# The heads' operand buffers moved into a pool of their own, released after the experts

## The chip, the cores and the metric

The kernel runs on one core of one Trainium2 chip. The metric is device time in microseconds of that core for one execution; the span of the profile, from its first to its last instruction (672.7 us for an execution of 674.4 us) is a little shorter. Five engines run side by side[...]: TensorE (PE, products), VectorE (DVE), ScalarE (ACT), GpSimd (POOL) and SyncE (SP, which here issues most DMA transfers).

## The reference

A gated linear attention (4 batches, 8 heads, 768 steps, head width 48, a complex gate) is followed by a mixture of 8 experts that sends each of the 3072 rows to one expert. Cut to what matters:

```python
def _attn_ref(q, k, v, a_re, a_im):
    mag = np.sqrt(a_re * a_re + a_im * a_im)
    scale = np.minimum(mag, 0.999) / (mag + 1e-06)
    a_re_n, a_im_n = (a_re * scale, a_im * scale)
    for t in range(S):                       # S = 768
        ...                                  # complex state, one step
        S_re, S_im = (new_re + kv, new_im)
        y[:, :, t] = np.einsum('bhd,bhde->bhe', q[:, :, t], S_re)

def _moe_ref(x, w_gate, w1, w2):             # x: 3072 rows of 384, from y
    logits = x @ w_gate
    expert_idx = np.argmax(logits, axis=1)
    ...                                      # gate_w: softmax weight of the chosen expert
    for e in range(E):                       # E = 8
        xe = x[expert_idx == e]
        h = np.maximum(xe @ w1[e], 0.0)      # 384 -> 1024
        out[mask] = gate_w[mask, None] * (h @ w2[e])
```

## The kernel before

Attention works in chunks of 128 steps. For each head it builds two operands, `KX` (keys and the chunk's decay) and `QX` (queries and a scaled diagonal), in a ring of six buffers each. The finished rows are collected in `xf`, given an expert and a place, and scattered by indirect DMA into `sorted_x` in HBM, expert by expert. The experts then load their rows from there, transpose them on VectorE, and multiply twice on TensorE. All of attention's tiles, the rings too, come from one pool, `one`:

```python
    with ExitStack() as att:
        one = att.enter_context(tc.tile_pool(name="one", bufs=1))
        ...
        def buf(nm, *shape):
            return one.tile([128, *shape], FP32, name=nm)
        ...
        packs = [buf(f"pk{i}", 2, C * CW) for i in range(3)]
        ...
        KXs = [buf(f"KX{i}", C * CW) for i in range(RING)]
        QXs = [buf(f"QX{i}", C, 128 + R2) for i in range(RING)]
        for i in range(RING):
            P.memset(KXs[i][R2:128, :], 0.0)
            P.memset(QXs[i][R2:128, :, :], 0.0)
```

The first 256 rows of expert 0 come from the first three batches, so they are complete before the last batch is. They are done early, between attention's last products: `early()` keeps their hidden values and results in operand buffers of heads that are through (`hq`, `hk`, `ys`), and writes the results to `out` from there:

```python
        def early(weights_in):
            w1t, w2t = weights(0)
            slots = [heads[B - 1, h][0] for h in (2, 3)]
            ...
            hq, hk = QXs[slots[0]].rearrange("p c w -> p (c w)"), KXs[slots[0]]
            ht = [...]                                   # eight slices of hq and hk
            ys = [KXs[slots[1]][:, i * DM:i * DM + DM] for i in range(EARLY // 128)]
            ...
            for i in range(EARLY // 128):
                ...                                      # products with w2 into o_ps
                o = act(DM, lambda i=i, o_ps=o_ps: A.activation(ys[i], o_ps, func=ACT.Copy, scale=gt_e[:, i, 0:1]), ...)
                pool_dma(1.1, lambda i=i: to_out(ys[i], out, to_e[:, i:i + 1]), [o, to])
```

The recorded operations (their source line is always that of one helper, L136) are put in an order by a scheduler of the kernel's own and emitted. Then the pool `one` is given back, and the experts open theirs. Expert 0 has only its late rows left there, 192 of its 448 places:

```python
    with ExitStack() as ms:
        xp = ms.enter_context(tc.tile_pool(name="xp", bufs=2))
        ...
        def load(e):
            xq = xp.tile([128, CAP // 32, R2], FP32, name="xq")
            c0 = first_tile(e) * 4
            for u in range(4):
                nc.sync.dma_start(xq[u * 32:u * 32 + 32, c0:], blocks(e, u, c0 * 32, CAP))   # L868
            return xq, notes_of(e)
        ...
        def turned(e, xq):
            xt = mp.tile([128, DT, CAP], FP32, name="xt")
            for d in range(DT):
                c0 = first_tile(e) * 4
                nc.vector.transpose(xt[:, d, c0 * 32:]..., xq[:, c0:, d * 32:d * 32 + 32])   # L885
            return xt

        xq, gt = load(0)
        mp = ms.enter_context(tc.tile_pool(name="mp", bufs=2))
        xt = turned(0, xq)
        for e in range(E):
            if e + 1 < E:
                xq, gt_next = load(e + 1)
            ...
            for f in range(FT):                          # first product and relu
                h = bank_of("h")[:, cols]
                for d in range(DT):
                    T.matmul(h, lhsT=w1t[:, d, f * 128:f * 128 + 128], rhs=xt[:, d, cols], ...)
                if f % 2:
                    nc.vector.tensor_scalar_max(ht[:, f, cols], h, 0.0)                      # L906
                else:
                    nc.scalar.activation(ht[:, f, cols], h, func=ACT.Relu)                   # L908
            if e + 1 < E:
                xt = turned(e + 1, xq)
            ...                                          # second product, results yo
            y = mp.tile([128, HALF], FP32, name="yh", bufs=2)
            nc.vector.tensor_scalar_mul(y, o[:, 0:HALF], gt[:, TT, 0:1])                     # L927
            to_out(y, halves, to[:, TT:TT + 1])
            if e + 3 < E:
                fetch(e + 3, nc.sync)                    # weights into the buffer of expert e
    banks.close()
```

A tile in a pool that takes over given-back memory waits for the users of the pool that it takes over from. TensorE's instructions keep their program order here (`T` is an in-order wrapper); VectorE's and ScalarE's in this part may be moved past each other when the program is built.

Of the kernel before, what the change touches and what calls it, by code (L numbers as in the profile page):

```python
# [9 lines left out]
FP32 = mybir.dt.float32  # L10
# [9 lines left out]
C = S // 128  # L20
# [6 lines left out]
CW = 128 + 2  # L27
R2 = 2 * D
RING = 6
# [110 lines left out]
def gateloop_then_moe(ctx, tc, q, k, a_re, a_im, v, wg, w1, w2, out):  # L140
# [142 lines left out]
    banks = ExitStack()  # L283
    bank = banks.enter_context(tc.tile_pool(name="bank", bufs=1, space=PSUM))
    two = bank.tile([128, 1024], FP32, name="two")
    ps = [two[:, 0:512], two[:, 512:]] + [bank.tile([128, 512], FP32, name=f"bank{i}") for i in range(2, 8)]

    with ExitStack() as att:
        one = att.enter_context(tc.tile_pool(name="one", bufs=1))
        V, A, T, Q = (InOrder(tc, e) for e in (nc.vector, nc.scalar, nc.tensor, nc.sync))  # L290
# [8 lines left out]
        def buf(nm, *shape):  # L299
            return one.tile([128, *shape], FP32, name=nm)  # L300
# [29 lines left out]
        P.memset(xfs[ROWS - 1][:, 0:XD + 1], 0.0)  # L330
        P.memset(xfs[ROWS - 1][:, XD + 1:WS], 4.0 * N)

        KXs = [buf(f"KX{i}", C * CW) for i in range(RING)]
        QXs = [buf(f"QX{i}", C, 128 + R2) for i in range(RING)]
        for i in range(RING):
            P.memset(KXs[i][R2:128, :], 0.0)
            P.memset(QXs[i][R2:128, :, :], 0.0)
# [773 lines left out]
```

## Time and profile before

| | |
|---|---|
| times of three runs | 676.70, 672.72, 676.45 us; median 676.45 |
| span of the profiled run | 672.7 us, 8204 instructions |
| busy TensorE / VectorE / ScalarE / GpSimd | 550.1 / 369.2 / 289.4 / 79.4 us |
| mean granted TensorE clock | 0.921 |
| moved by DMA | 89.81 MB, mean 134 GB/s |

The page gives the span in 40 slices with a digit for each engine's busy share in tenths, and groups of instructions: line, engine, operation, written tile <- read tiles, count, then busy time, mean ns of one, and the idle time of the engine just ahead of them with what ended it. In the timeline a row is the start, the duration, the engine, the line, the operation with its tiles, and in brackets the idle time ahead of it and what released it. `SPq` and `POOLq` stand for the issue of a DMA transfer by SyncE or GpSimd, not for its movement of data. Every product of fp32 tiles appears as two matmuls.

### The profile page before, as it was taken

To read this page: it belongs to the slowest core of one execution; us is meant where nothing else is said; L and a number is where in the kernel's file an instruction comes from. 1 tells how busy PE (TensorE), PEld (TensorE's weight loads), DVE (VectorE), ACT (ScalarE), POOL (GpSimd) and SP (SyncE) were. 2 spreads that over 40 slices of the span, in tenths; PEclk is the share of its full clock that TensorE was granted. 3 is DMA by queue.
4 is the path that set the end of the run, shared out by engine and by line. 5 is a ranking of instruction groups with operands and counts; after the bars stand their busy time and mean duration, and the time that the engine had idled before them with its cause. 6 is when DMAs were issued, how large, how long until landed. Compare 5 with 4: busy or idle time off the path is not lost. (4 is left out here: it accounts for less than half of the span.)

```text
span 672.7 us, 8204 instructions
## 1 busy us (share of the span) xinstructions
PE 550.1 (82%) x2594; PEld 336.1 (50%) x2594; DVE 369.2 (55%) x782; ACT 289.4 (43%) x940; POOL 79.4 (12%) x96
## 2 busy tenths in 40 slices
PE   1550388968897778977998689999999999999993
PEld 0220245645564455654666375555555565655552
DVE  5999999999999999999533021201111201110010
ACT  6555588688998697766642001000000001010100
POOL 9100000000004004004003101110101020101111
PEclk9666599979999698979999989999999999999997
DMA  8694857277635646287397156354434441000000
GB/s 258 154 246 114 205 133 200 65 197 172 159 95 143 166 122 184 58 202 184 93 366 287 34 131 157 126 151 136 142 116 137 97 120 75 24 18 24 9 12 29
DMA packets 77635, 89.81 MB, mean 134 GB/s; under 512 B 25341, under 2 KB 67343, under 8 KB 75536
## 3 DMA queue, kind: packets, MB, share of 16 engines
q1 hardware_dynamic: 74000, 79.33, 43.6%
q0 software_dynamic: 3584, 9.87, 4.1%
q8 instruction: 22, 0.36, 0.2%
q14 instruction: 29, 0.24, 0.1%
HBM read 54.31 MB, written 16.63 MB: 105 GB/s over the span
## 5 line engine op out<-in xcount | busy, mean ns | idle before, releaser
L136 PE MATMUL bank<-xt,big 128*128 128x448 f32 (+1 forms) x384 | 137.7, 520 | 8.1 <-DVE xt L885 8.1
L136 PE MATMUL bank<-big,ht 128*128 128x384 f32 (+1 forms) x608 | 136.8, 420 | 0.0
L136 PE MATMUL bank<-QX,KX 128*128 128x224 f32 (+1 forms) x384 | 95.5, 382 | 34.7 <-DMA KX<-pk 26.1
L136 PEld LDWEIGHTS bank<-big,ht 128*128 128x128 f32 (+1 forms) x608 | 84.5, 168 | 53.6 <-issue 7.0
L136 PEld LDWEIGHTS bank<-xt,big 128*128 128x128 f32 x384 | 72.6, 194 | 70.5 <-issue 61.6
L136 PEld LDWEIGHTS bank<-QX,KX 128*128 128x128 f32 x384 | 69.3, 207 | 51.6 <-issue 34.7
L136 ACT ACTIVATE big<-big 128x576 f32<-128x576 f32 (+3 forms) x77 | 68.6, 904 | 15.6 <-DVE big L136 14.2
L906 DVE TENSOR_SCALAR ht<-bank 128x448 f32<-128x448 f32 (+1 forms) x32 | 18.9, 591 | 100.0 <-PE bank L136 100.0
L136 ACT ACTIVATE QX<-diag,KX 96x48 f32<-96x48 f32 x280 | 72.6, 336 | 1.6 <-DMA KX<-pk 1.6
L908 ACT ACTIVATE ht<-bank 128x448 f32<-128x448 f32 (+1 forms) x32 | 16.6, 518 | 130.5 <-PE bank L136 120.5
L785 POOL DMA_INDIRECT sorted_x<-xf,slot x24 | 30.4, 1265 | 316.7 <-DMA big<-in_a_im_dram 154.6
L136 PE MATMUL two<-big,ident 128*128 128x512 f32 (+1 forms) x112 | 42.0, 527 | 30.1 <-ACT big L136 25.7
L136 PE MATMUL bank<-ak,vb 128*48 128x224 f32 (+1 forms) x384 | 54.8, 369 | 14.0 <-ACT ak L136 12.1
L136 DVE TENSOR_TENSOR big<-big,big 128x576 f32<-128x576 f32 (+3 forms) x86 | 65.0, 766 | 0.8
L919 ACT ACTIVATE yo<-bank,gt 128x384 f32<-128x384 f32 x15 | 8.7, 582 | 122.4 <-PE bank L136 122.4
L136 DVE TENSOR_TENSOR big<-big 128x288 f32<-128x288 f32 (+5 forms) x108 | 55.2, 519 | 6.2 <-ACT big L136 5.5
L269 POOL DMA_INDIRECT out_dram<-yo,to x22 | 21.3, 970 | 239.4 <-ACT yo L919 183.5
L136 DVE TENSOR_TENSOR ak<-bank,causal 128x256 f32<-128x256 f32 x96 | 39.9, 418 | 15.9 <-PE bank L136 15.3
L136 PEld LDWEIGHTS two<-big,ident 128*128 128x128 f32 x112 | 21.9, 229 | 50.0 <-issue 32.7
L136 PE MATMUL bank<-QX,st 128*48 128x224 f32 (+1 forms) x320 | 44.0, 355 | 0.8 <-ACT st L136 0.8
L136 PE MATMUL bank<-across,ys 128*128 128x104 f32 x192 | 38.2, 290 | 4.4 <-ACT xf L136 2.3
L136 ACT ACTIVATE ys<-bank 128x224 f32<-128x224 f32 (+1 forms) x96 | 32.4, 344 | 18.1 <-PE bank L136 17.6
(126 smaller groups left out, 556.4 us busy)
## 6 DMA issues: line engine op xcount, KB each, us to landing
big<-in_moe_w_dram SPq DMA_DIRECT2D x16, 1536.0 KB
KX<-pk SPq DMA_DIRECT2D x44, 146.2 KB
QX<-pk SPq DMA_DIRECT2D x44, 144.0 KB
sorted_x<-xf SPq DMA_DIRECT2D x8, 731.5 KB
xq<-sorted_x SPq DMA_DIRECT2D x28, 168.0 KB
big<-in_a_re_dram SPq DMA_DIRECT2D x16, 288.0 KB
big<-in_a_im_dram SPq DMA_DIRECT2D x16, 288.0 KB
qt<-in_q_dram SPq DMA_DIRECT2D x12, 384.0 KB
```

Source lines behind the costliest of these rows:

```text
L136: return lambda *a, **kw: self.tc.keep_in_program_order(f(*a, **kw))
L269: move = nc.gpsimd.indirect_dma_start(out=rows, out_offset=bass.IndirectOffsetOnAxis(ap=index, axis=0), in_=y, in_offset=None, bounds_chec ...
L785: move = nc.gpsimd.indirect_dma_start(out=sorted_x[:, :], out_offset=bass.IndirectOffsetOnAxis(ap=slot[:, i:i + 1], axis=0), in_=xfs[(b * ...
L906: nc.vector.tensor_scalar_max(ht[:, f, cols], h, 0.0)
L908: nc.scalar.activation(ht[:, f, cols], h, func=ACT.Relu)
L919: nc.scalar.activation(y, o, func=ACT.Copy, scale=gt[:, i, 0:1])
```

## The change

The rings of `KX` and `QX` go into a pool of their own, opened ahead of attention's pool and closed only after the experts (with the PSUM banks, `banks.close()`). It is meant so that late rows' buffers in the experts' pools wait only for attention's other tiles, not for the operands, in which the early rows' results still stand. No instruction is added or taken away in the source.

```diff
@@ -285,6 +285,9 @@
     two = bank.tile([128, 1024], FP32, name="two")
     ps = [two[:, 0:512], two[:, 512:]] + [bank.tile([128, 512], FP32, name=f"bank{i}") for i in range(2, 8)]
 
+
+    ring_of = banks.enter_context(tc.tile_pool(name="ring", bufs=1))
+
     with ExitStack() as att:
         one = att.enter_context(tc.tile_pool(name="one", bufs=1))
         V, A, T, Q = (InOrder(tc, e) for e in (nc.vector, nc.scalar, nc.tensor, nc.sync))
@@ -330,8 +333,8 @@
...
-        KXs = [buf(f"KX{i}", C * CW) for i in range(RING)]
-        QXs = [buf(f"QX{i}", C, 128 + R2) for i in range(RING)]
+        KXs = [ring_of.tile([128, C * CW], FP32, name=f"KX{i}") for i in range(RING)]
+        QXs = [ring_of.tile([128, C, 128 + R2], FP32, name=f"QX{i}") for i in range(RING)]
         for i in range(RING):
             P.memset(KXs[i][R2:128, :], 0.0)
             P.memset(QXs[i][R2:128, :, :], 0.0)
```

## The prediction

> **What bounds the kernel now.** I read the busy times by slice first, then one table by stretch of time for the hand-over from attention to experts, then the waits, then the timeline there. Part 2 of the page says that two engines take turns: VectorE is at 9 tenths or more up to about half the span, TensorE after it.
>
> ```profile
> PE   1550388968897778977998689999999999999993
> DVE  5999999999999999999533021201111201110010
> PEclk9666599979999698979999989999999999999997
> ```
>
> Counted from 1, each slice is 16.8 us long; slice 23 shows a 6 for TensorE, the lowest digit between the middle of the span and its last slice. The table by stretch puts edges to it (columns: stretch and its length, busy us of each engine with instruction counts, granted clock, DMA share, GB/s):
>
> ```profile
> 368.00:381.00 13.00, 11.88 (x41) 6.98 (x40) 1.00 (x3) 1.35 (x3) 0.97 (x1) 1.00 0.05 17
> 381.00:389.10 8.10, 0.03 (x1) 0.00 (x0) 0.41 (x2) 0.58 (x1) 0.97 (x1) 0.77 0.26 61
> 389.10:391.60 2.50, 2.48 (x8) 2.48 (x9) 0.68 (x4) 0.03 (x1) 0.00 (x0) 0.50 0.84 171
> 391.60:398.70 7.10, 7.10 (x43) 7.10 (x42) 1.07 (x3) 1.30 (x4) 0.00 (x0) 0.95 0.28 37
> 420.00:662.00 242.00, 241.91 (x861) 135.63 (x860) 33.94 (x70) 21.75 (x39) 26.19 (x27) 1.00 0.29 84
> ```
>
> From 381.0 to 389.1 TensorE does nothing; in the 2.5 us after that it has half its clock; from 420 to 662 it is busy for 241.91 of 242 us. So whatever starts the experts earlier ends the kernel earlier. Who holds it back: first the row of part 5 for the experts' first product (its last column: idle before, and what ended it), then the waits of the DMA queue and of all engines from 366 to 410.
>
> ```profile
> L136 PE MATMUL bank<-xt,big 128*128 128x448 f32 (+1 forms) x384 | 137.7, 520 | 8.1 <-DVE xt L885 8.1
> ```
>
> ```profile
> SPq L868 <- DMA out_dram<-KX,to_e: 43.6, 2, 39.8
> ...
> DVE xt L885 <- DMA xq<-sorted_x: 13.1, 1, 13.1
> ```
>
> The chain is: product waits for the transposed rows xt, xt for the load xq, and the load for the DMA that writes the early rows' result out of a KX buffer. That store has nothing to do with the rows being loaded. The timeline has the moments:
>
> ```profile
> 375.12 0.42 DVE L136 TENSOR_SCALAR KX<-two 128x256 f32<-128x256 f32 x1 [4.97 <-PE two L136]
> 378.93 2.10 PE L136 MATMUL two<-big,KX 128*128 128x384 f32 x6
> 381.92 0.97 POOL L269 DMA_INDIRECT out_dram<-KX,to_e  x1 [2.85 <-ACT KX L136]
> 384.82 1.78 SPq L868 DMA_DIRECT2D xq<-sorted_x  x4
> 388.69 0.90 DVE L885 STREAM_TRANSPOSE xt<-xq 128x192 f32<-128x192 f32 x3 [13.15 <-DMA xq<-sorted_x]
> 389.12 9.60 PE L136 MATMUL bank<-xt,big 128*128 128x192 f32 x48 [8.10 <-DVE xt L885]
> 399.03 1.69 DVE L885 STREAM_TRANSPOSE xt<-xq 128x448 f32<-128x448 f32 x3
> 406.56 18.31 PE L136 MATMUL bank<-xt,big 128*128 128x448 f32 x48
> 406.68 0.42 DVE L927 TENSOR_SCALAR yh<-bank,gt 128x192 f32<-128x192 f32 x1 [5.96 <-PE bank L136]
> ```
>
> The second early store is issued at 381.92, and the loads of xq start at 384.82, 2.9 us later; 3.87 us from there to the transposes, 0.43 more to the product.
>
> **What the Trainium skill says.** (1) "TensorE: Matmul & The Clock Gate", Part 1: the clock halves after an idle window of about 3.4 us and comes back after about that much sustained work. The trace agrees: 0.77 over the 8.1 us of idleness, 0.50 in the 2.5 us after it. (2) "DMA: Bandwidth & Descriptors", Anatomy of one DMA (SWDGE): some 2 us are fixed for a DMA issued by GpSimd, most of it the receipt of the write. Here 2.9 us from issue to the waiter, of which 0.97 us are GpSimd's own. (3) The TensorE page again, Architectural detail: VectorE's queue is strictly first in, first out. That matters for the part of the change that I count as a cost; nothing in the timeline above contradicts it.
>
> **The change part by part.** I laid the two built programs side by side, engine by engine, with what each instruction waits for. Every engine has as many instructions as before, and their order is the same except for four on VectorE.
>
> (a) Memory. KX and QX take 51,072 bytes of each partition. Before they lie behind the other attention tiles, after in front of them. The experts' tiles move up by the same 51,072 bytes, so that they lie on the same attention tiles as before (rows on the old state, packing and value tiles; the half-row result on the edge of xf). They never lay on KX or QX: the wait came from giving back one pool as a whole, with every user of it.
>
> (b) Waits removed. The first xq load, the first transpose, the first expert product and the first relu lose the wait for the two early stores and for the activation that fills KX. What the load keeps: the six last scatters into sorted_x (it reads what they write) and attention's last uses of other tiles. The last scatter is issued at 365.54; from 368 to 370 the DMA moves 0 GB/s, so it has landed by about 368. Loads start there, and with the same 3.87 us xq is in by 372.2. VectorE must first do its last early relu, 375.12 + 0.42; then three transposes in 0.90 us: xt is there by 376.5. TensorE ends the early rows at 378.93 + 2.10 = 381.03. So xt is 4.5 us ahead and the product follows at once: **-8.1 us**.
>
> (c) Clock. With no idleness the experts' first stage runs at full clock. In the timeline its relus come every 0.975 us once the clock is back (392.90 on VectorE to 398.75, six stages in 5.85 us). Eight stages then take 7.8 us; before they took 389.12 to 398.55, 9.43 us: **-1.6 us**.
>
> (d) Order on VectorE. The scale of expert 0's half rows (yh) stands ahead of the three transposes for expert 1 now; before it stood behind them. yh waits for the last product of expert 0, and expert 1's first product waits for the first transpose. Before, the transposes ran at 399.03, hidden; after, they lie between two products. yh begins 0.12 us after the last product (406.68 against 406.56) and takes 0.42; a transpose 0.60 (the median of the 21 of this width); 0.1 us from a transpose's end to the product (388.69 + 0.335 for the shorter form = 389.03, product at 389.12). Sum 0.12 + 0.42 + 0.60 + 0.1 = 1.2 us. The second and third transposes come 0.55 us apart (1.69 for three), the products on each third take 2 x 0.375 = 0.75 us, so only the first one shows: **+1.2 us**. It happens at expert 0 alone.
>
> (e) The start. The initial clears of KX and QX on GpSimd, and the first load of q, exchange a wait on the setup tiles. Those are done by 3.5 us, and the engines reach these instructions at 6.2 us or later: 0.
>
> Sum: -8.1 - 1.6 + 1.2 = -8.5 us. The median before is 676.45, which gives 667.95. The three times before are 672.72, 676.45 and 676.7; their mean, 675.3, gives 666.8. I choose 667.5.
>
> **The rivals.** *The next wait takes over.* If the scatters land late, or the loads queue behind the 9.4 MB of weights that share the queue, xt comes after 381. For: the loads stand behind those in program order. Against: DMA share is 0.30 from 366 to 368 and 0 after it, and 4.5 us are in hand. Were xq to land at 385, the product would start at 385.4: 3.7 us of the idleness gone, the slow clock still there after 4.4 us without work, and (d) to pay: -2.5, some 674.
> *The order on VectorE costs more.* A stall of 1.2 us could pull the clock down for a window: another 1.7 us (3.4 us at half clock), some 669. Against: before, TensorE's stall of 1.02 us ahead of the early product at 364.36 leaves the clock at 1.00.
> *The gain is lost later.* The weights of expert 3 are loaded into buffers that expert 0 frees; all that moves earlier by the same amount. For losing it a wait would have to exist after 420, and TensorE lacks only 0.09 us there, with DMA share 0.29. Nothing to lose it to; this would make 676.
>
> **Range and chances.** The change in time is -8.5, with -10 if the stall hides and -2.5 if the loads come late. The larger uncertainty is the 4 us between runs of one program. So 663.5 to 670.5. Two per cent of 676.45 is 13.5 us: faster by that would need more than all of the idleness and the slow clock together (9.7 us), 0.04; slower would need a new wait of over 22 us, 0.02; within, 0.94.
>
> **What would show it.** Right: the wait of L868 on the store from KX is gone and one on the scatters stands in its place; xq starts near 368, xt near 375.5; TensorE's idleness of 8.1 before the first xt product is gone, and an idleness of about 1.2 us, ended by a VectorE transpose, appears near 397; clock 1.00 from 381 on; the last product ends about 8.5 us earlier. Wrong: xq starting later than 377, the clock at 0.5 after 381, or an idle TensorE behind expert 1.

## The result, and the profile after

| | median of four runs, us | lowest to highest |
|---|---|---|
| before | 675.56 | 672.72 to 676.70 |
| after | 665.62 | 664.63 to 666.24 |

The ratio is 0.9858, with a 95% interval of 0.9822 to 0.9893: 9.9 us less by these medians. Two further comparisons, each beside its own runs of the kernel before, gave 0.9864 (0.9844 to 0.9885) and 0.9859 (0.9835 to 0.9882), that is 9.2 and 8.8 us. The prediction was 667.5, 8.5 us less.

First, part 2 of the page of after, in the same 40 slices:

```profile
PE   1541288968899478968998999999999999999993
...
PEclk9865599998999689988999999999999999999997
```

TensorE's hole of slice 23 has become a 9, as in all slices behind it up to the last. The table by stretch (columns as before: stretch and length, busy us of TensorE, its weight load, VectorE, ScalarE and GpSimd, the granted clock, the DMA share, GB/s) covers the end of the early rows, expert 0's first stage, the join to expert 1 and the long rest:

```profile
379.10:381.60 2.50, 2.50 (x15) 2.23 (x14) 0.00 (x0) 0.91 (x2) 0.86 (x1) 1.00 0.00 0
381.60:388.00 6.40, 6.40 (x40) 6.27 (x39) 1.39 (x4) 0.99 (x3) 0.11 (x1) 1.00 0.08 31
...
395.00:400.00 5.00, 3.85 (x17) 2.00 (x14) 2.13 (x6) 0.54 (x1) 0.97 (x1) 1.00 0.73 246
410.00:652.00 242.00, 242.00 (x862) 135.77 (x860) 33.81 (x69) 21.73 (x39) 26.24 (x27) 1.00 0.29 84
```

The idleness ahead of expert 0 is gone and the clock is 1.00 throughout. Of the stretches shown, only that from 395 to 400 has a gap: 5.00 - 3.85 = 1.15 us. The row of part 5 for the experts' first product says what ends it, and the waits of the DMA queue say what the load of xq waits for now:

```profile
L136 PE MATMUL bank<-xt,big 128*128 128x448 f32 (+1 forms) x384 | 136.1, 514 | 1.1 <-DVE xt L888 1.1
```

```profile
SPq L871 <- DMA sorted_x<-xf,slot: 27.2, 1, 27.2
```

L871 is the xq load, which was L868 before. It no longer waits for the store out of KX, only for the scatters into the rows that it reads. The timeline of after:

```profile
364.36 0.97 POOL L788 DMA_INDIRECT sorted_x<-xf,slot  x1 [2.81 <-issue]
367.86 1.78 SPq L871 DMA_DIRECT2D xq<-sorted_x  x4
...
374.64 0.90 DVE L888 STREAM_TRANSPOSE xt<-xq 128x192 f32<-128x192 f32 x3 [0.27 <-issue]
...
377.75 2.10 PE L136 MATMUL two<-big,KX 128*128 128x384 f32 x6
379.69 7.96 PE L136 MATMUL bank<-xt,big 128*128 128x192 f32 x48
380.74 0.97 POOL L269 DMA_INDIRECT out_dram<-KX,to_e  x1 [2.85 <-ACT KX L136]
387.49 8.07 PE L136 MATMUL bank<-big,ht 128*128 128x384 f32 x48
...
395.68 0.42 DVE L930 TENSOR_SCALAR yh<-bank,gt 128x192 f32<-128x192 f32 x1 [7.64 <-PE bank L136]
396.02 1.69 DVE L888 STREAM_TRANSPOSE xt<-xq 128x448 f32<-128x448 f32 x3
...
396.71 5.53 PE L136 MATMUL bank<-xt,big 128*128 128x448 f32 x14 [1.15 <-DVE xt L888]
```

The load is issued 13 us ahead of the store it used to wait for (367.86 against 380.74), and the transposed rows are there at 375.54, 4.2 us before TensorE asks for them. At 395.68 VectorE scales the half rows first and transposes second; expert 1's product waits 1.15 us for that.

One difference between the two profiles is not the change's. Expert 0's product starts 9.43 us sooner, but 1.06 us of that was already there at the first scatter of the last group (356.12 before, 355.06 after), in a part of the program that does the same work. Over all profiles below this moment lies anywhere between 355.06 and 358.64. So I measure from it. The table gives, for each profiled execution, the start of the first scatter of that group, and the times from it to expert 0's first product, through expert 0's first stage, from its second stage to expert 1's first product, and from there to the end of the span. Each is the difference of two starts in the timeline; the last stretch ends with the span. The kernels that follow "after" are explained with the experiments.

| kernel | first scatter | to expert 0 | its first stage | second stage to expert 1 | to the end | scatter to expert 1 |
|---|---|---|---|---|---|---|
| before | 356.12 | 33.00 | 9.43 | 8.01 | 266.1 | 50.44 |
| before, again | 356.69 | 33.19 | 9.50 | 8.00 | 266.1 | 50.69 |
| after | 355.06 | 24.63 | 7.80 | 9.22 | 266.2 | 41.65 |
| after, second time | 356.50 | 24.73 | 7.80 | 9.22 | 266.4 | 41.75 |
| after, third time | 357.26 | 24.69 | 7.80 | 9.22 | 266.4 | 41.71 |
| wait put back | 355.65 | 32.03 | 10.28 | 8.01 | 266.4 | 50.32 |
| only KX moved | 355.64 | 27.42 | 7.91 | 8.00 | 266.1 | 43.33 |
| only QX moved | 357.17 | 33.21 | 9.98 | 8.01 | 266.2 | 51.20 |
| before, kept busy | 356.50 | 33.14 | 7.91 | 8.00 | 266.7 | 49.05 |
| order fixed | 356.92 | 24.72 | 7.80 | 8.01 | 266.2 | 40.53 |
| order fixed, again | 358.64 | 24.72 | 7.80 | 8.01 | 266.4 | 40.53 |
| four areas, own schedule | 355.94 | 29.17 | 9.55 | 8.01 | 266.3 | 46.73 |
| four areas, old schedule | 356.81 | 22.35 | 7.80 | 8.00 | 266.2 | 38.15 |

From before to after: 33.1 to 24.7 is -8.4, 9.47 to 7.80 is -1.7, 8.0 to 9.22 is +1.2, and nothing behind it: -8.9 us together (50.57, the mean of the two profiles of before, to 41.70). The medians of the three comparisons gave 8.8 to 9.9 us.

### The profile page after: what moved, and what is told of

It reads as the page before. It is cut to its first block, busy times and chain, and to the rows that moved or that the text cites. A ratio compares the mean times of both kernels' runs of the same rounds, so it can differ in the third digit from the quotient of the medians.

```text
span 662.9 us, 8204 instructions
## 1 busy us (share of the span) xinstructions
PE 547.0 (83%) x2594; PEld 334.5 (50%) x2594; DVE 368.9 (56%) x782; ACT 289.4 (44%) x940; POOL 79.0 (12%) x96
## 5 line engine op out<-in xcount | busy, mean ns | idle before, releaser
L136 PE MATMUL bank<-xt,big 128*128 128x448 f32 (+1 forms) x384 | 136.1, 514 | 1.1 <-DVE xt L888 1.1
L136 PEld LDWEIGHTS bank<-xt,big 128*128 128x128 f32 x384 | 71.1, 190 | 63.3 <-issue 60.8
```

What stands on the lines that cost most here:

```text
L136: return lambda *a, **kw: self.tc.keep_in_program_order(f(*a, **kw))
```

## The experiments

My theory: the one wait that the pool's giving back put on xq made all of the idleness, the idleness made the slow clock, and the order on VectorE costs 1.2 us. The rivals: the memory's places or the changed program itself make the gain; the clock has nothing to do with it; the 1.2 us stall is made up later.

### The changed kernel again, and its VectorE order mended

> The changed kernel itself, as the measure for the others on this chip. 665.6 us, within 1 us. Its profile is a second sample of the attention phase: in the first, TensorE ended the early rows 1.2 us earlier than in the kernel before (379.85 against 381.03), though nothing in that phase was changed. If that is chance, this run's early rows end anywhere from 379.5 to 381.5; if the new addresses make attention faster, near 379.8 again.

> The changed kernel with the transposes for the next expert kept ahead of the half rows' scale on VectorE, by program order. Theory (the stall of 1.15 us between expert 0 and expert 1 is the price of the new order): that idleness of TensorE is gone and the time is 1.1 us below the changed kernel's, 664.5. Rival (the products would wait for something else there, such as the load of xq for expert 1 or the results' PSUM bank): a stall of about the same length with another releaser, 665.6.

The second kernel keeps the transposes and the scale in program order, so that the transposes run while expert 0's second products do:

```diff
+        V = InOrder(tc, nc.vector)
-                nc.vector.transpose(xt[:, d, c0 * 32:]..., xq[:, c0:, d * 32:d * 32 + 32])
+                V.transpose(xt[:, d, c0 * 32:]..., xq[:, c0:, d * 32:d * 32 + 32])
-            nc.vector.tensor_scalar_mul(y, o[:, 0:HALF], gt[:, TT, 0:1])
+            V.tensor_scalar_mul(y, o[:, 0:HALF], gt[:, TT, 0:1])
```

Measured: 666.37 us (665.25 to 668.35) for the changed kernel, 665.28 us (664.7 to 667.01), ratio 0.9848 (0.9833 to 0.9863), for the mended one. Its timeline:

```profile
389.44 8.07 PE L136 MATMUL bank<-big,ht 128*128 128x384 f32 x48
...
389.92 1.69 DVE L136 STREAM_TRANSPOSE xt<-xq 128x448 f32<-128x448 f32 x3
...
397.45 10.79 PE L136 MATMUL bank<-xt,big 128*128 128x448 f32 x28
397.64 0.42 DVE L136 TENSOR_SCALAR yh<-bank,gt 128x192 f32<-128x192 f32 x1 [6.03 <-PE bank L136]
```

The transposes start 7.5 us before the product that needs them (389.92 against 397.45), and the product has no idle time ahead of it. In the table the second stage falls from 9.22 to 8.01 us, and nothing behind it gives the 1.21 us back. By the medians it is 1.1 us here and 0.6 in the last comparison below; these intervals alone do not separate the two kernels.

The second profile of the changed kernel settles the question of chance: its last early product ends at 381.39 (379.29 + 2.10), later than the 381.03 of the kernel before, so the 1.2 us in the first profile do not come with the new addresses.

### The wait put back

> The changed kernel, pools and addresses and all, with one thing put back: the four loads of expert 0's late rows wait for the two early stores again. Theory (the wait alone made the difference): idleness of about 8 us before the first xt product, half clock after it, no stall at expert 1, and the time of the kernel before, 675.5. Rival (addresses or the new pool order speed up attention, by the 1.2 us seen): about 674.3. Second rival (the gain had another source): stays near 666.

The changed kernel, with its pools and addresses; only expert 0's loads of xq wait for the two early stores again:

```diff
-                nc.sync.dma_start(xq[u * 32:u * 32 + 32, c0:], blocks(...))
+                move = nc.sync.dma_start(xq[u * 32:u * 32 + 32, c0:], blocks(...)).ins
+                if e == 0:
+                    for store in early_stores:
+                        tc.add_manual_dep(move, store.name, ...)
```

Measured: 675.49 us (672.74 to 676.71), ratio 0.999 (0.9978 to 1.0002). Waits of the DMA queue, timeline, and a table by stretch with the clock:

```profile
SPq L871 <- DMA out_dram<-KX,to_e: 10.4, 1, 10.4
```

```profile
381.03 0.97 POOL L269 DMA_INDIRECT out_dram<-KX,to_e  x1 [2.85 <-ACT KX L136]
383.66 3.83 SPq L871 DMA_DIRECT2D xq<-sorted_x  x8
387.20 0.90 DVE L892 STREAM_TRANSPOSE xt<-xq 128x192 f32<-128x192 f32 x3 [12.34 <-DMA xq<-sorted_x]
387.68 10.45 PE L136 MATMUL bank<-xt,big 128*128 128x192 f32 x48 [7.55 <-issue]
```

```profile
380.14:382.34 2.20, 0.00 (x0) 0.00 (x0) 0.00 (x0) 0.58 (x1) 0.97 (x1) 1.00 0.00 0
382.34:387.68 5.34, 0.00 (x0) 0.03 (x1) 0.48 (x2) 0.00 (x0) 0.00 (x0) 0.50 0.52 129
387.68:392.58 4.90, 4.90 (x15) 4.90 (x16) 0.78 (x3) 0.33 (x1) 0.00 (x0) 0.50 0.63 100
392.58:397.96 5.38, 5.38 (x34) 5.38 (x34) 0.71 (x2) 0.99 (x3) 0.00 (x0) 1.00 0.00 0
```

The whole gain is gone, with the new addresses kept. From the scatter to expert 1 it is 50.32 us, against 50.57 before. So the places of the tiles are worth nothing that these runs can tell from zero, and the wait is worth all of it. Within the stretch the parts differ a little from the kernel before: the load starts 2.6 us after the store's start instead of 2.9, expert 0 starts 1.1 us earlier in the table, and the slow clock then costs 0.8 us more. (The order on VectorE went back to the old one here too, which the 8.01 in the table shows; the bracket after the product says "issue" where it had waited for the transposes.)

### One ring moved alone

> Only KX in the pool of its own; QX stays in attention's pool. The built program shows that the first xq load then no longer waits for the two stores out of KX, but for the last early product that reads QX. Theory (the load starts when the last reader in attention's pool is through): that product ends near 378.5, so xq starts at about 378.5 instead of 367.9, the expert's product at about 382.8, TensorE idle for 2.9 us before it; the old order on VectorE is back, so no stall at expert 1 (-1.15). 3 us of idleness may or may not pull the clock down (0 to +1.6): 667.5 to 669. Rival (the stores alone were the wait, QX is of no matter): idleness 0, 664.5.

> Only QX in the pool of its own; KX stays, so the wait for the stores out of KX stays as well, and VectorE has its old order. Theory: the time of the kernel before, 675.5, TensorE idle for about 8 us ahead of the first xt product. Rival (moving a large operand buffer ahead of the other attention tiles makes attention faster): 674.3.

The edits to the changed kernel, one for each:

```diff
-        QXs = [ring_of.tile([128, C, 128 + R2], FP32, name=f"QX{i}") for i in range(RING)]
+        QXs = [buf(f"QX{i}", C, 128 + R2) for i in range(RING)]     # only KX moved
```
```diff
-        KXs = [ring_of.tile([128, C * CW], FP32, name=f"KX{i}") for i in range(RING)]
+        KXs = [buf(f"KX{i}", C * CW) for i in range(RING)]          # only QX moved
```

Measured: only KX 668.52 us (666.93 to 670.41), ratio 0.9899 (0.9884 to 0.9914); only QX 675.89 us, ratio 0.9983 (0.9968 to 0.9998). For KX alone, the waits and the timeline:

```profile
SPq L871 <- PE two L136: 10.6, 1, 10.6
```

```profile
376.46 2.10 PE L136 MATMUL two<-big,QX 128*128 128x384 f32 x6
...
378.69 1.81 SPq L871 DMA_DIRECT2D xq<-sorted_x  x4
...
383.06 8.07 PE L136 MATMUL bank<-xt,big 128*128 128x192 f32 x48 [2.57 <-DVE xt L888]
```

The table by stretch around this hole:

```profile
380.00:382.00 2.00, 0.49 (x2) 0.00 (x0) 0.00 (x0) 0.58 (x1) 0.61 (x1) 1.00 0.71 130
382.00:384.00 2.00, 0.94 (x6) 0.94 (x7) 1.09 (x5) 0.00 (x0) 0.35 (x1) 1.00 0.38 109
384.00:386.00 2.00, 2.00 (x14) 2.00 (x14) 0.36 (x1) 0.33 (x1) 0.00 (x0) 1.00 1.03 216
```

With only KX out of the way, the next holder in the same pool steps in: the load starts 0.13 us after the last product that reads QX (376.46 + 2.10 = 378.56). That leaves 2.57 us of idleness, but the clock stays at full rate and the first stage takes 7.91 us. With only QX moved, the load waits for the KX store as ever:

```profile
SPq L871 <- DMA out_dram<-KX,to_e: 44.5, 2, 40.7
```

Its interval ends just under 1, but its profile shows nothing that got shorter (51.20 us from scatter to expert 1, against 50.44 and 50.69), so I make nothing of the 0.17%.

### TensorE kept busy while it waits

> The kernel before, with 11 products (128x384, identity by a block of weights) added ahead of expert 0's late rows. Nobody reads their results; they fill TensorE's idle 8 us without being waited for by anything but expert 0's first product, and take 11 x 2 x 0.323 = 7.1 us at full clock, so the chain of store, load and transposes still sets when expert 0 starts. It separates the clock's share from the idleness itself. Theory (the slow start of expert 0 is the clock, and the clock follows idleness): granted clock 1.00 near 389, the first stage in 7.8 us rather than 9.4 to 10.3, and the time 1.6 to 2.5 us below the kernel before: 673.0 to 674.0. Rival (the slow first stage comes from cold loads or waits of expert 0, not from idleness): stage still 9.4 us or more, 675.5.

> The kernel before once more, for a second profile of the hand-over. In the first one the first stage of expert 0 took 9.43 us after 8.1 us of idleness; where the wait was put back into the changed kernel it took 10.28 after 7.5 us. If the clock comes back at a moment that differs from run to run, this one lies anywhere from 9.2 to 11.2 us; if the idleness alone sets it, 9.4 again.

The kernel before, with eleven products of no use ahead of expert 0, into an area of PSUM that nobody reads at that time:

```diff
+        for i in range(11):
+            T.matmul(ps[1][:, 0:384], lhsT=ident, rhs=weights(0)[1][:, i % FT, :], start=True, stop=True)
```

Measured: 674.35 us, ratio 0.9969 (0.9956 to 0.9981): -2.2 us by the medians, and 1.3 to 3.0 us less by the interval of the ratio. The second kernel named is the kernel before once more, for one profile (second line of the table). Its first stage took 9.50 us, which fits both of the readings named; the last section decides between them. The timeline of the busy one, and the stretch in which its expert 0 starts, with the clock at 1.00:

```profile
385.08 1.78 SPq L868 DMA_DIRECT2D xq<-sorted_x  x4
...
389.21 0.90 DVE L885 STREAM_TRANSPOSE xt<-xq 128x192 f32<-128x192 f32 x3 [13.40 <-DMA xq<-sorted_x]
389.64 8.07 PE L136 MATMUL bank<-xt,big 128*128 128x192 f32 x48 [0.32 <-DVE xt L885]
```

```profile
388.00:390.00 2.00, 1.68 (x7) 0.80 (x6) 0.79 (x3) 0.00 (x0) 0.00 (x0) 1.00 0.29 26
```

The wait is as long as before (33.14 us from scatter to product), but the first stage takes 7.91 us instead of 9.47. This separates the clock's part from the wait's: about 1.6 us by the trace, by products that compute nothing.

### A version that beats both: four areas for the early rows' products

With the hole gone, TensorE waits in the early rows for relus that have to clear one of two areas of PSUM before it may write there again. I tried four areas, on top of the mended order. First with the scheduler told of them:

```diff
-            readers = [state["sum"], state["sum"]]
+            readers = [state["sum"], state["sum"], used["at", 0], used["at", 1]]
-                h = two[:, f % 2 * 512:f % 2 * 512 + EARLY]
+                h = ps[f % 4][:, 0:EARLY]
...                                                   # readers[f % 2] -> readers[f % 4]
```

> The changed kernel with VectorE's order kept, and the early rows' first products turning through four PSUM areas instead of two (the two attention score banks are free by then). TensorE stands still for 2.9 us in the early rows of the changed kernel, each time for a relu that empties one of two areas. Theory: with four areas most of that goes, and nothing else bounds the hand-over (xt is 4.5 us ahead): 2 us below the order-only kernel, 663.3. Rival (the last scatters come later in the new order, so that xq or xt becomes the bound): a new idleness ahead of the first xt product, and 665 or more.

Measured: 670.16 us (667.69 to 672.06), ratio 0.9901 (0.9879 to 0.9924), worse than the mended order alone (0.9848). Waits of the DMA queue, and timeline:

```profile
SPq L872 <- PE bank L136: 8.8, 1, 8.8
```

```profile
379.71 0.17 PE L136 MATMUL bank<-oh,ones 128*128 128x8 bf16 x1
379.74 0.89 PE L136 MATMUL two<-big,KX 128*128 128x384 f32 x2
...
379.95 0.81 SPq L872 DMA_DIRECT2D xq<-sorted_x  x2
```

The scheduler, given more freedom, put one 0.17 us product of the router's counts at the very end, behind nearly all of the early rows. It reads `oh`, which is a tile of attention's pool, so the load of xq waited for it. The wait that the change removed came back under another name, 4.2 us of idleness and a first stage of 9.55 us with it. In the second try the scheduler's account stays as it was, so that the order of instructions is the mended kernel's and only the areas differ (the middle edit of the diff alone):

> The version with the early rows' first products spread over four areas of PSUM instead of two, and this time with the scheduler's own account of the areas left as it was, so that every engine gets its instructions in the order of the in-order version and only the areas differ. If TensorE's waits for the relus of two units back (QX on VectorE 1.7 us in 2, KX on ScalarE 0.5, QX on ScalarE 0.4, KX on VectorE 0.3 in the profiles, about 2.9 us in all) cost the path that sets the end, early rows end 2 to 2.5 us sooner, expert 0 follows without idle time, and the time is 2 to 2.5 us below the in-order version of the same call (about 663). If TensorE is then held by the second products' wait for the same relus, or by the next scatters, the gain is under 0.7 us and the page shows idleness moved from the first products to L137-type waits.

> The in-order version once more, beside the four areas: about 665.3 (664.5 to 667), the stall ahead of expert 1's product absent; 0.5 to 1.5 us below the changed kernel of the same call if the 1.15 us stall was on the path, no difference if it was made up later.

> The changed kernel once more, as the yardstick of this call: 665.5 to 667, a stall of about 1.15 us ahead of expert 1's first product.

Measured on one chip, beside 675.86 for before: changed kernel 667.05 us (665.55 to 667.73), mended order 666.41 us (663.85 to 667.34), four areas 664.09 us (662.86 to 664.30), ratio 0.982 (0.9799 to 0.9842). TensorE's waits from 340 to 384, of the mended order and then of the four areas:

```profile
PE two L136 <- DVE QX L136: 1.7, 2, 1.0
...
PE two L136 <- ACT KX L136: 0.5, 1, 0.5
PE two L136 <- ACT QX L136: 0.4, 1, 0.4
PE two L136 <- DVE KX L136: 0.3, 1, 0.3
```

```profile
PE bank L136 <- ACT QX L136: 0.8, 1, 0.8
PE two L136 <- ACT QX L136: 0.4, 1, 0.4
```

Waits of 2.9 us have become 1.2, and the stretch from the scatter to expert 0 falls from 24.72 to 22.35 us, without a new idle time ahead of expert 0's product. That is 2.4 us in the trace and 2.3 in the medians. The listed waits account for 1.7 of it. The timelines account for the other 0.7, as an estimate: the rows have two waits left of five, a product without a wait starts some 0.16 us before the modelled end of the one ahead of it, and a group of four takes 1.03 us without a wait and 1.13 behind one, so three waits fewer save 3 x 0.26 = 0.8 us more.

## Why the prediction was right, step by step

- **(b) The wait, -8.1.** The mechanism is shown: putting back that wait restores the old time. Its size is -8.4 us in the mean of five profiles. The kernel before was idle for 8.10 and 8.40 us in its two profiles, 8.25 in the mean. The other 0.16 us the prediction left out: without a wait, expert 0's product starts at 379.69, ahead of the modelled end of the last early product (377.75 + 2.10 = 379.85). The load was expected near 368 and started at 367.86. The margin of xt was put at 4.5 us and is 4.2: no DMA ended the wait of the transposes, which follow VectorE's last early relu by 0.27 us.
- **(c) The clock, -1.6.** The first stage takes 7.80 us as computed from the relus' spacing, against 9.43 and 9.50: -1.7. The busy version of before gives about the same by an independent way. The size rests on luck, which the prediction did not say: other idle holes cost 1.75 (four areas, own schedule), 2.2 (only QX) and 2.5 us (wait put back) in the same stage.
- **(d) The order on VectorE, +1.2.** 9.22 against 8.01 is +1.21, and the idle time stands where it was said to, behind yh and ahead of expert 1. Mending the order removes it. Why the program as built has the new order in the changed kernel, and the old one with one ring moved or the wait put back (8.00 and 8.01 in the table), no run here shows.
- **(a) and (e), nothing.** The new addresses with the old wait give the old time, to within the interval of 1.5 us less to 0.1 us more.
- **The sum, -8.5**, is -8.9 by the trace. The medians of the three comparisons gave -9.9, -9.2 and -8.8; that the first has more is within its interval, and attention's own spread, seen in the table's first column, is large enough for it.

Of the rivals, *the order costs more* fell: in the 1.15 us stall the clock is 1.00. *The gain is lost later* fell: from expert 1's first product to the end it is 266.1 to 266.7 us in all thirteen profiles, so every microsecond saved ahead of it reached the end. *The next wait takes over* did not happen in the changed kernel, but the experiments show how near it is: with only KX moved, the products that read QX take over, and with another schedule a count of the router does. The rival had named other causes, late scatters or loads behind the weights, and neither came. That expert 0's product started at 385.11 with the four areas' own schedule, near the rival's 385.4, is chance.

## What to carry to other kernels

When a pool is given back as a whole, its heirs wait in these runs for the last user in it, whatever they overlap. Find the tile with the latest user and let it live in a pool of its own, and then ask who is the next latest: here it was QX, and under another schedule a tiny tile of the router. Measure such a change from a landmark just ahead of it to one just behind it: profiles of the same kernel agreed to 0.25 us or better between the landmarks, while the whole times of one program in one comparison spread over 1.4 to 5.8 us.

## What the runs showed of the hardware that I had not expected

The price of an idle hole is not set by its length: in expert 0's first stage a hole of 4.19 us cost 1.75 us (four areas, own schedule), one of 8.10 us 1.63 (before) and one of 7.55 us 2.48 (wait put back). The moments at which the clock changed follow from stretches of 1 us. For the kernel before:

```profile
385.00:386.00 1.00, 0.00 (x0) 0.00 (x0) 0.00 (x0) 0.00 (x0) 0.00 (x0) 0.72 0.10 18
386.00:387.00 1.00, 0.00 (x0) 0.00 (x0) 0.00 (x0) 0.00 (x0) 0.00 (x0) 0.50 0.68 153
...
392.00:393.00 1.00, 1.00 (x7) 1.00 (x6) 0.10 (x1) 0.00 (x0) 0.00 (x0) 0.87 1.25 177
```

A clock of 0.72 in the first row is 0.44 us at full and 0.56 at half clock, so it fell at 385.44; the last row in the same way has it back at 392.26. TensorE's clock fell to half between 2.2 us (wait put back) and about 4.9 us (before, again) after its last product. It came back between 3.1 us (before) and 4.9 us (wait put back) after the first new one, and half of that time is what the first stage lost: 1.6 to 2.5 us.

What the length leaves open shows when all five profiles are laid side by side. From the fall to the return it took 3.41 us (four areas, own schedule), 6.83 (both profiles of before) or 10.24 (wait put back, only QX moved): one, two and three times 3.41. Worked out in the same way, the 208 changes of the clock from 0 to 410 us in the thirteen profiles that stretches of 1 us resolve lie on a grid with steps of 3.413 us, each profile with its own start, to 0.02 us. So in these runs the clock changes only at beats of 3.41 us, and what a hole costs depends on where it falls between them.

A hole of 2.57 us cost no clock at all (only KX moved), though another had lost its clock 2.2 us after the last product. The grid of the profile with only KX moved has a beat at 382.09, an estimate from its earlier changes, which divides the hole into 1.60 and 0.97 us; the 2.2 us of the other lay in one step, from 378.93 (382.34 less one step) to 382.34. This fits "TensorE: Matmul & The Clock Gate", Part 1 of the Trainium skill, which calls the window of 3413 ns free-running. It does not fit the prediction's reading that an idle window of about 3.4 us comes first: here 2.2 us of idleness were enough. How much idleness in a step is too much stays open; in attention a step with only 1.2 us of it also ended in a fall (143.15 to 146.57, only KX moved).
